# Attention and a squared-ReLU feed-forward: both feed-forward products by Strassen's seven on quarters, two batches a unit

## Chip, cores, metric

One core of one Trainium2 chip. The metric is the time of one execution on the device in microseconds (us), the median of several runs (4 of the kernel before). "PE" is TensorE, "DVE" VectorE, "ACT" ScalarE, "POOL" GpSimd, "SP" SyncE, as in the profile.

## The reference, cut

```python
# q, k, v: 8 batches, 12 heads, 448 rows, 64 columns, float32
q_n, k_n = rmsnorm(q, g_q), rmsnorm(k, g_k)
attn = softmax(q_n @ k_n.T / sqrt(64))
x = (attn @ v)                      # heads side by side: 3584 x 768
h = maximum(x @ w_in, 0)            # 768 x 2048, float64 weights
out = (h * h) @ w_out               # 2048 x 768, float64 weights
```

## The kernel before

A batch's attention goes by pairs of heads (6 pairs, 4 steps each). The feed-forward of batch b-1 is cut into pieces that are issued on PE between the steps of batch b; the last batch's runs alone at the end. The weights arrive as float64 words and are turned into float32 by passes on ACT, POOL and DVE during the first batch and the beginning of the second (the last pass starts at 232.8 us, when the feed-forward already runs); they then stay in SBUF.

```python
for f in range(NF):                                   # first product, 16 tiles of w_in
    ps = banks[6 + f % 2][:, 0:S]
    for c in range(NC):
        nc.tensor.matmul(ps, lhsT=w_in_sb[:, c, ts(f, P)], rhs=xT[c], start=c == 0, stop=c == NC - 1)
    nc.scalar.activation(h[:, at : at + S], ps, AF.Relu)
    nc.gpsimd.tensor_tensor(out=full, in0=full, in1=full, op=ALU.mult)     # (cut: the odd 64 columns)
for n, tt in enumerate(tiles):                        # second product
    for half in range(2):
        ps = banks[6 + half][:, 0:HALF]
        for f in range(NF):
            nc.tensor.matmul(ps, lhsT=h2[f][:, ts(n, P)], rhs=w_out_sb[:, f, ts(half, HALF)], ...)
        # one copy to y, then the store

def convert(k):                                       # one weight chunk
    join_words(k - 1)      # DVE, three passes
    load_weights(k + 3)    # SP
    split_words(k)         # ACT, POOL clamp, ACT, POOL or ACT
```

Of the kernel before, what the change touches and what calls it, by code (L numbers as in the profile page):

```python
# [17 lines left out]
P = 128  # L18


NJ = 4
# [52 lines left out]
def program(ctx, tc, q, k, v, g_row, moe_w_in, moe_w_out, out, shift):  # L74
# [7 lines left out]
    NF = DFF // P  # L82
    HALF = DM // 2
    REST = S % P
    assert 2 * D == P and DM == H * D and B % 2 == 0 and 2 * REST == P and HALF <= 512

# [5 lines left out]
    psum = ctx.enter_context(tc.tile_pool(name="psum", bufs=1, space=bass.MemoryType.PSUM))  # L92

# [4 lines left out]
    w_in_sb = const.tile([P, NC, DFF], F32, name="w_in_sb")  # L98
    w_out_sb = const.tile([P, NF, DM], F32, name="w_out_sb")


# [6 lines left out]
    loaded, values, squared, normal, turned, weights, sums, dens, xts = {}, {}, {}, {}, {}, {}, {}, {}, {}  # L108
# [60 lines left out]
    def turn(i):  # L169

        qn, kn, _ = normal[i]
        qT = att.tile([P, S], F32, name="qT", tag="qT")
        kT = att.tile([P, S], F32, name="kT", tag="kT")
        for x, (dst, rows) in enumerate(((qT, qn), (kT, kn))):
            tr = banks[2 + x][:, 0:S]
            for j in range(NJ):
                nc.tensor.transpose(tr[:, ts(j, CP)], rows[:, j].rearrange("p h d -> p (h d)"), ident[:CP, :CP])  # L177
            if x == 0:
                nc.vector.tensor_scalar(  # L179
                    out=dst, in0=tr, scalar1=g, scalar2=None, op0=ALU.mult  # L180
                )
            else:
                nc.scalar.copy(dst, tr)
        turned[i] = qT, kT
# [5 lines left out]
    def weigh(i, m):  # L190

        if shift:
            return weigh_shifted(i, m)
        new_weights(i, m)
        qT, kT = turned[i]
        scs = [banks[2 * (m % 2) + e][:CP, 0:S] for e in range(2)]
        for e, sc in enumerate(scs):
            r = ds(e * D, D)
            nc.tensor.matmul(sc, lhsT=kT[r, ts(m, CP)], rhs=qT[r, :], start=True, stop=True)  # L199
        for e, sc in enumerate(scs):  # L200
            nc.scalar.activation(  # L201
                weights[i, e, m], sc, AF.Exp, scale=normal[i][2][:, 2 * m + e : 2 * m + e + 1]
            )
        add_up(i, m)

    def add_up(i, m):

        if m == 0 or pairs[i][0] == 0:
            return
        for e in range(2):  # L210
            if m == 1:
                sums[i, e] = att.tile([CP, S], F32, name="sum", tag="sum", bufs=2)
            so_far = weights[i, e, 0] if m == 1 else sums[i, e]
            engine = nc.gpsimd if e == 0 else nc.vector
            engine.tensor_tensor(out=sums[i, e], in0=so_far, in1=weights[i, e, m], op=ALU.add)  # L215

    def weigh_shifted(i, m):
# [4 lines left out]
        qT, kT = turned[i]  # L222
        for e in range(2):
            r = ds(e * D, D)
            sc = banks[2 * e][:CP, 0:S]
# [3 lines left out]
            w = att.tile([CP, S], F32, name="w", tag="w", bufs=1)  # L229
            nc.scalar.activation(w, sc, AF.Exp, bias=nmax)  # L230
            tr = banks[2 * e + 1][:CP, 0:S].rearrange("p (n c) -> p n c", n=NJ)
# [7 lines left out]

    def attend(i, m):  # L240
# [5 lines left out]
        b, c = pairs[i]  # L246
        vt = values[i]
        alone = b == 0
        av = banks[4 + i % 2][:, 0:S]
        den = banks[6 + i % 2 if alone else 5 - i % 2][:, 0:S]  # L250
        for e in range(2):
            nc.tensor.matmul(  # L252
                av[ds(e * D, D), :], lhsT=vt[:, e, m, :], rhs=weights[i, e, m],
                start=m == 0, stop=m == NJ - 1,
            )
        for e in range(2):
            wT = weights.pop((i, e, m))
            if alone:
# [7 lines left out]
        if m == (NJ - 1 if alone else 1):  # L266
# [9 lines left out]

    def finish(i):

        b, c = pairs[i]
        if c == 0:  # L280
            xts[b] = [None] * NC
        xT = ffn_p.tile([P, S], F32, name="xT", tag="xT", bufs=NC + 2)
        nc.vector.tensor_tensor(
            out=xT, in0=banks[4 + i % 2][:, 0:S], in1=dens.pop(i), op=ALU.mult
        )
        xts[b][c] = xT
        del turned[i], normal[i], values[i]



    left = {}

    def out_tiles(b):
        return range(0, S // P) if b % 2 == 0 else range(S // P, 2 * S // P)

    def ffn_pieces(b):
        return NF * 2 + len(out_tiles(b)) * 2 * (NF // 4)

    def ffn(b):

        xT = xts.pop(b)
        at = 0 if b % 2 == 0 else REST
        h2 = []
        for f in range(NF):
            ps = banks[6 + f % 2][:, 0:S]
            for c in range(NC):
                nc.tensor.matmul(  # L307
                    ps, lhsT=w_in_sb[:, c, ts(f, P)], rhs=xT[c],
                    start=c == 0, stop=c == NC - 1,
                )  # L310
                if c == NC // 2 - 1:
                    yield
            if f % 2 == 0:
                two = ffn_p.tile([P, 2, REST + S], F32, name="h2", tag="h2", bufs=NF // 2)
            h = two[:, f % 2]
            nc.scalar.activation(h[:, at : at + S], ps, AF.Relu)  # L316
            if b % 2 == 0:
                rest = ffn_p.tile([P, REST], F32, name="rest", tag="rest", bufs=NF)
                full = h[:, 0 : S - REST]
                over = h[:, S - REST : S]  # L320
                nc.gpsimd.tensor_tensor(out=full, in0=full, in1=full, op=ALU.mult)  # L321
                nc.gpsimd.tensor_tensor(out=rest, in0=over, in1=over, op=ALU.mult)
                left[f] = rest
            else:
                full = h[:, REST : REST + S]
                nc.gpsimd.tensor_tensor(out=full, in0=full, in1=full, op=ALU.mult)  # L326
                nc.gpsimd.tensor_copy(out=h[:, 0:REST], in_=left.pop(f))
            h2.append(h)
            yield
        tiles = out_tiles(b)  # L330
        for n, tt in enumerate(tiles):
            y = ffn_p.tile([P, DM], F32, name="y", tag="y")
            for half in range(2):
                ps = banks[6 + half][:, 0:HALF]
                for f in range(NF):
                    nc.tensor.matmul(  # L336
                        ps, lhsT=h2[f][:, ts(n, P)], rhs=w_out_sb[:, f, ts(half, HALF)],
                        start=f == 0, stop=f == NF - 1,
                    )
                    if f % 4 == 3 and f < NF - 1:  # L340
                        yield
                if half == 0:
                    nc.vector.tensor_copy(out=y[:, ts(half, HALF)], in_=ps)  # L343
                else:
                    nc.scalar.copy(y[:, ts(half, HALF)], ps)  # L345
                    store(b, tt, y)
                yield

    def store(b, tt, y):

        pos = P * tt
        while pos < P * (tt + 1):
            odd, col = divmod(pos, S)
            j, p = divmod(col, CP)
            n = min(CP - p, P * (tt + 1) - pos)
            rows = out[ds((b - b % 2 + odd) * S, S), :].rearrange("(p j) c -> j p c", j=NJ)
            nc.sync.dma_start(rows[j, p : p + n], y[pos - P * tt : pos - P * tt + n, :])
            pos += n



    def weight_chunks():

        n = DFF // 4
        for blk in range(4):
            for c in range(NC):
                yield w_in_sb[:, c, ts(blk, n)], moe_w_in[ts(c, P), :], blk * n
        for half in range(2):
            for f in range(NF):
                yield w_out_sb[:, f, ts(half, HALF)], moe_w_out[ts(f, P), :], half * HALF  # L370

    chunks = list(weight_chunks())
    words = {}

    def load_weights(k):
        if k >= len(chunks):
            return
        dst, rows, col = chunks[k]
        n = dst.shape[1]
        if rows.dtype == F32:  # L380
            nc.sync.dma_start(dst, rows[:, col : col + n])
            return

        early = n == DFF // 4 or k % 2 and k < len(chunks) - NF // 2
        tag, bufs = ("h2", NF // 2) if early else ("y", 2)
        words[k] = ffn_p.tile([P, n, 2], U32, name="words", tag=tag, bufs=bufs)
        nc.sync.dma_start(
            words[k].rearrange("p n w -> p (n w)"), rows.bitcast(U32)[:, 2 * col : 2 * (col + n)]
        )
# [9 lines left out]
    def split_words(k):  # L399
        if k not in words:  # L400
            return
        low, high = words[k][:, :, 0], words[k][:, :, 1]
# [6 lines left out]
        if k < 4 * NC:  # L409
            nc.gpsimd.tensor_scalar(  # L410
                out=low, in0=low.bitcast(F32), scalar1=-(2.0**23), scalar2=1.0,
# [5 lines left out]
    def join_words(k):  # L417
        if k not in words:
            return
# [119 lines left out]
```

## Time and profile before

| | before |
|---|---|
| median | 1717.55 us (4 runs, 1715.78 to 1717.78) |
| span of the profiled run | 1714.3 us |
| first feed-forward matmul | 128.2 us |
| feed-forward alone at the end | from 1552.9 us |

PE is the bound from 128 us on. A line of the page's fifth part reads: source line, engine, operation, output <- inputs, shapes, count, then busy us and mean ns of one, then the engine's idle time before these instructions and who ended it. A matmul of the program is two records in the trace.

### The profile page before, as it was taken

The numbers are of one execution on the slowest core, as the hardware profiler recorded it, in microseconds if no ns is written. First come the engines' busy times: TensorE is split into PE (matmuls) and PEld (weight loads), VectorE is DVE, ScalarE is ACT, GpSimd is POOL, SyncE is SP. The second block draws the span as 40 slices with busy tenths as digits, with TensorE's granted clock in tenths as the row PEclk, the third lists the DMA queues.
The fourth block names the chain that finished last, engine by engine and source line by source line (L and its number), as shares of the span: only waits on it lengthen the run. The fifth ranks groups of instructions, "written<-read, shape, count | busy, mean of one in ns | idle before, by whom it ended". The sixth has DMA issues, their size and how long they took to land.

```text
span 1714.3 us, 14444 instructions
## 1 busy us (share of the span) xinstructions
PE 1649.2 (96%) x5516; PEld 773.9 (45%) x5516; DVE 489.6 (29%) x616; ACT 455.5 (27%) x829; POOL 559.4 (33%) x564
## 2 busy tenths in 40 slices
PE   5879899999999999999999999999999999999998
PEld 2224345444554445534455344444455444454554
DVE  4886731311223122222112222131121312221000
ACT  5666531222113222132111322122211222111100
POOL 5765531333113332233312343133321333211200
PEclk9989999999999999999999999999999999999999
DMA  5533421100011000010010101110001100000000
GB/s 189 187 109 116 122 66 35 42 17 16 26 36 42 16 16 26 26 42 17 17 35 26 42 16 33 35 42 16 16 26 33 43 16 17 15 15 10 0 19 20
DMA packets 80211, 70.24 MB, mean 41 GB/s; under 512 B 47876, under 2 KB 69380, under 8 KB 80132
## 3 DMA queue, kind: packets, MB, share of 16 engines
q1 hardware_dynamic: 80128, 69.23, 13.7%
q8 instruction: 45, 0.74, 0.2%
q14 instruction: 34, 0.28, 0.1%
q10 hardware_dynamic: 4, 0.00, 0.0%
HBM read 58.20 MB, written 11.01 MB: 40 GB/s over the span
## 4 chain that ended last, share of the span: by engine, by line
PE 89%; issue 4%; DVE 4%; POOL 2%; ACT 1%; DMA 0%; POOLq 0%; DVEq 0%; ACTq 0%; SPq 0%
PE bank L336 34%; PE bank L307 32%; PE bank L199 9%; PE bank L252 9%; PE bank L177 2%; PE bank L263 2%; POOL rr L151 1%; DVE w_in_sb L427 1%; DVE sum L215 1%; DVE w_in_sb L423 1%; DVE qT L179 1%; PE bank L259 0%; DVE w_out_sb L427 0%; DMA words<-in_moe_w_out_dram 0%; POOL words L404 0%
## 5 line engine op out<-in xcount | busy, mean ns | idle before, releaser
L307 PE MATMUL bank<-xT,w_in_sb 128*128 128x448 f32 x1536 | 599.9, 545 | 7.6 <-ACT h L316 6.2
L336 PE MATMUL bank<-w_out_sb,h 128*128 128x384 f32 x1792 | 593.9, 489 | 0.0
L336 PEld LDWEIGHTS bank<-w_out_sb,h 128*128 128x128 f32 x1792 | 335.4, 190 | 254.0 <-issue 31.4
L307 PEld LDWEIGHTS bank<-xT,w_in_sb 128*128 128x128 f32 x1536 | 286.6, 191 | 311.7 <-issue 279.1
L201 ACT ACTIVATE wT<-bank,rr 112x448 f32<-112x448 f32 x384 | 222.7, 631 | 547.3 <-PE bank L199 547.3
L199 PE MATMUL bank<-qT,kT 64*112 64x448 f32 x768 | 203.2, 609 | 35.8 <-DVE qT L179 35.2
L252 PE MATMUL bank<-wT,vt 112*64 112x448 f32 x768 | 192.7, 583 | 0.0
L151 POOL TENSOR_TENSOR rr<-ms,minus_half 112x16 f32<-112x16 f32 x48 | 140.4, 2925 | 131.5 <-DVE ms L147 125.4
L316 ACT ACTIVATE h<-bank 128x448 f32<-128x448 f32 x128 | 69.4, 543 | 422.3 <-PE bank L307 422.3
L215 DVE TENSOR_TENSOR sum<-wT 112x448 f32<-112x448 f32 x42 | 26.9, 641 | 539.7 <-PE bank L263 534.6
L215 DVE TENSOR_TENSOR sum<-sum,wT 112x448 f32<-112x448 f32 x84 | 79.8, 950 | 348.3 <-ACT wT L201 348.3
L215 POOL TENSOR_TENSOR sum<-wT 112x448 f32<-112x448 f32 x42 | 66.9, 1592 | 307.4 <-PE bank L263 307.4
L215 POOL TENSOR_TENSOR sum<-sum,wT 112x448 f32<-112x448 f32 x84 | 95.9, 1142 | 194.5 <-ACT wT L201 193.5
L274 DVE RECIPROCAL rden<-bank 128x448 f32<-128x448 f32 x48 | 141.7, 2951 | 6.8 <-PE bank L259 5.6
L326 POOL TENSOR_TENSOR h<-h 128x448 f32<-128x448 f32 x64 | 59.8, 934 | 215.1 <-ACT h L316 215.1
L199 PEld LDWEIGHTS bank<-qT,kT 64*112 64x112 f32 x768 | 55.5, 178 | 152.7 <-issue 93.8
L321 POOL TENSOR_TENSOR h<-h 128x384 f32<-128x384 f32 x64 | 54.2, 847 | 170.4 <-ACT h L316 170.4
L252 PEld LDWEIGHTS bank<-wT,vt 112*64 112x64 f32 x768 | 39.2, 137 | 132.2 <-issue 129.3
L343 DVE COPY y<-bank 128x384 f32<-128x384 f32 x28 | 15.4, 549 | 263.2 <-PE bank L336 263.2
L345 ACT COPY y<-bank 128x384 f32<-128x384 f32 x28 | 13.4, 479 | 216.6 <-PE bank L336 204.0
L146 DVE TENSOR_REDUCE ms<-squares 112x8 f32<-112x512 f32 x96 | 61.3, 679 | 4.4 <-ACT squares L138 4.4
L138 ACT ACTIVATE squares<-qk 112x512 f32<-112x512 f32 x96 | 55.4, 627 | 2.3 <-DMA qk<-in_q_dram 1.4
(41 smaller groups left out, 629.8 us busy)
## 6 DMA issues: line engine op xcount, KB each, us to landing
words<-in_moe_w_in_dram SPq DMA_DIRECT2D x24, 512.0 KB, 4.4
words<-in_moe_w_out_dram SPq DMA_DIRECT2D x32, 384.0 KB, 3.4
qk<-in_q_dram SPq DMA_DIRECT2D x48, 224.0 KB, 2.9
qk<-in_k_dram SPq DMA_DIRECT2D x96, 112.0 KB, 3.3
vt<-in_v_dram SPq DMA_DIRECT2D x48, 224.0 KB, 2.8
out_dram<-y SPq DMA_DIRECT2D x8, 336.0 KB, 2.7
out_dram<-y SPq DMA_DIRECT2D x8, 288.0 KB, 2.6
out_dram<-y SPq DMA_DIRECT2D x8, 240.0 KB, 2.8
```

The lines of the kernel that those rows point to most:

```text
L138: nc.scalar.activation(squares[x], loaded[i][:, x], AF.Square)
L146: nc.vector.tensor_reduce(out=ms[:, ts(x, 2 * NJ)], in_=squares, axis=AX.X, op=ALU.add)
L151: nc.gpsimd.tensor_tensor(out=rr.rearrange("p x r -> p (x r)"), in0=ms, in1=minus_half.to_broadcast([CP, 4 * NJ]), op=ALU.pow,)
L199: nc.tensor.matmul(sc, lhsT=kT[r, ts(m, CP)], rhs=qT[r, :], start=True, stop=True)
L201: nc.scalar.activation(weights[i, e, m], sc, AF.Exp, scale=normal[i][2][:, 2 * m + e : 2 * m + e + 1])
L215: engine.tensor_tensor(out=sums[i, e], in0=so_far, in1=weights[i, e, m], op=ALU.add)
L252: nc.tensor.matmul(av[ds(e * D, D), :], lhsT=vt[:, e, m, :], rhs=weights[i, e, m], start=m == 0, stop=m == NJ - 1,)
L274: nc.vector.reciprocal(out=rden, in_=den)
L307: nc.tensor.matmul(ps, lhsT=w_in_sb[:, c, ts(f, P)], rhs=xT[c], start=c == 0, stop=c == NC - 1,)
L316: nc.scalar.activation(h[:, at : at + S], ps, AF.Relu)
L326: nc.gpsimd.tensor_tensor(out=full, in0=full, in1=full, op=ALU.mult)
L336: nc.tensor.matmul(ps, lhsT=h2[f][:, ts(n, P)], rhs=w_out_sb[:, f, ts(half, HALF)], start=f == 0, stop=f == NF - 1,)
```

## The change

Intent: cut the work of PE. Both operands of a product are split in quarters; Strassen's form (seven products of sums of quarters, in place of eight) cuts 1/8 of the matmuls. The first product is split along the model dimension, the middle dimension and, as rows, into *two batches*: so a unit is two batches. The second works on blocks of the middle dimension, four in a unit, and adds to accumulators in SBUF. The sums of weight quarters ("forms") are made once, written to scratch memory in DRAM and streamed back for every unit. Beside the feed-forward, attention keeps PSUM banks 0 to 3 and the products rotate through 4 to 7. The diff, cut to its core:

```diff
-    w_in_sb = const.tile([P, NC, DFF], F32, name="w_in_sb")
-    w_out_sb = const.tile([P, NF, DM], F32, name="w_out_sb")
+    in_forms = [dram.tile([P, NK, 7, P], F32, ...) for p in range(NF // 2)]
+    out_forms = [dram.tile([P, 8, HALF], F32, ...) for t in range(NF // 2)]
+    ORDER = [("P1", 0, True, "11", "11"), ("P5", 1, True, "S1", "T1"), ("P2", 2, True, "12", "21"),
+        ("P6", 0, False, "S2", "T2"), ("P4", 3, True, "22", "T4"), ("P3", 1, False, "S4", "22"),
+        ("P7", 0, False, "S3", "T3")]          # name, bank, first in it, left and right operand
+    def first_products(u, p, hid):
+        for name, role, first, left, right in ORDER:
+            for c in range(NK):
+                nc.tensor.matmul(roles[role][:, 0:S], lhsT=w_sb[:, c, IN.index(left), :], rhs=forms[u, c][right], ...)
+            # P1, P5, P6, P4: ACT copies the bank; P2, P3, P7: hidden(bank, copy)
+    def hidden(dst, ps, part, op):
+        nc.vector.tensor_tensor(out=dst, in0=ps, in1=part, op=op)
+        nc.scalar.activation(dst, dst, AF.Relu)
+        nc.gpsimd.tensor_tensor(out=dst, in0=dst, in1=dst, op=ALU.mult)
+    def second_products(u, blk, hid, accs):
+        for half in range(2):                  # the leftover tile: 64 rows of each batch
+            for a in range(2):
+                for t in range(2):
+                    nc.tensor.matmul(roles[half][:, 0:HALF], lhsT=flat[a][:, t, ds(FULL, P)], ...)
+            add_to(accs[-1][:, ts(half, HALF)], ps, blk == 0)
+            yield 2 * COST_OUT
+        for dst, left, right, op in (s1, ...), (s2, ...), (s3, ...), (s4, ...):
+            nc.gpsimd.tensor_tensor(out=dst, in0=left, in1=right, op=op)
+        # three row tiles x ORDER x two matmuls; DVE adds each bank to its accumulator
+    def join_words(n):
+        # ... the three DVE passes ...
+        if form == 3:
+            make_weight_forms(...)             # four adds on POOL, then the write to DRAM
     def convert(n):
         join_words(n - 1)
-        load_weights(k + 3)
+        load_weights(n + 4)
         split_words(n)
     # ... in the loop over pairs i and steps n:
-        turn(i + 1)                            # both transposes at step 2
+        if n % 2 == 0 and i < last:
+            turn(i + 1, n // 2)                # qT at step 0, kT at step 2
```

Not shown: batch 1's sums of the softmax go to PE matmuls, as batch 0's did; from batch 2 on the scores use two banks and not four; the loads and the normalization of q and k are issued earlier. All 64 weight pieces are now converted during the attention of batches 0 and 1, with which no feed-forward can be interleaved.

## The prediction

> **What bounds the kernel now.** I read the page of the kernel before first: busy shares, slices, chain.
>
> ```profile
> PE 1649.2 (96%) x5516; PEld 773.9 (45%) x5516; DVE 489.6 (29%) x616; ACT 455.5 (27%) x829; POOL 559.4 (33%) x564
> PE   5879899999999999999999999999999999999998
> ...
> PE bank L336 34%; PE bank L307 32%; PE bank L199 9%; PE bank L252 9%; PE bank L177 2%; PE bank L263 2%; POOL rr L151 1%; DVE w_in_sb L427 1%; DVE sum L215 1%; DVE w_in_sb L423 1%; DVE qT L179 1%; PE bank L259 0%; DVE w_out_sb L427 0%; DMA words<-in_moe_w_out_dram 0%; POOL words L404 0%
> ```
>
> TensorE is full from the fourth slice on, and two thirds of the chain are the two feed-forward products (L307, L336). A busy PE is not a PE at its peak, so I looked for its pace where nothing disturbs it: the chain in order of time ends with one batch's feed-forward alone.
>
> ```profile
> 1552.87 72.36 PE bank L307 x192
> 1625.23 82.57 PE bank L336 x256
> ```
>
> That is 72.36/192 = 0.3769 us for 448 columns and 82.57/256 = 0.3225 us for 384: 2 x 448/2.4 GHz is 373 ns, so this is the floor plus 3 ns. (Each matmul of the program is two records.) By the counts of the page's costliest groups (1536 of L307, 1792 of L336; odd batches have four row tiles, even ones three) all feed-forward costs 1536 x 0.3769 + 1792 x 0.3225 = 579 + 578 = 1157 us.
>
> The windows view tells two stages apart: two whole batches in the middle, then the first 320 us in steps of 20, of which three follow.
>
> ```profile
> 429.31:838.32 409.01, 405.04 (x1362) 190.09 (x1361) 98.90 (x115) 95.41 (x171) 128.51 (x124) 1.00 0.10 27
> ...
> 60.00:80.00 20.00, 15.75 (x70) 4.94 (x68) 18.37 (x22) 13.06 (x24) 15.05 (x12) 0.91 0.52 169
> 80.00:100.00 20.00, 16.93 (x76) 5.42 (x76) 18.58 (x24) 14.08 (x26) 14.51 (x15) 0.91 0.64 209
> ```
>
> In the middle PE is busy 99% and DVE, ACT and POOL 24 to 31%. The period of 409 us for twelve head pairs and two batches of feed-forward (289.3 us) leaves (409.0 - 289.3)/12 = 9.97 us of attention for a pair. In the first 128 us there is no feed-forward to lay between: attention of batch 0 runs beside the conversion of the weights, and DVE is the bound (18.4 of 20 us). The scores' last step of pairs 1 to 6 begins at 41.03, 57.61, 73.22, 89.29, 105.36 and 123.34 in the timeline, some 16.1 us a pair. The first feed-forward matmul is at 128.17.
>
> **What the Trainium skill says.** "TensorE: Matmul & The Clock Gate", section "Wait — 56ns, not 53.3ns?": back-to-back warm matmuls start N/2.4 GHz plus about 2.5 ns apart; the 3 ns above agree, so fewer matmuls are fewer microseconds, one for one. The same page, "What's actually happening": after an idle window of about 3.4 us the array runs at half its clock until busy again about as long. The trace agrees: after 3.07 us idle at 105.36 four score matmuls took 1.84 us in place of 1.01. "DMA: Bandwidth & Descriptors", "Measured": one 1 MB transfer takes 6.15 us, 341 GB/s. The kernel before has none over 512 KB, but a slice of its first 150 us reaches 353 GB/s. "GPSIMD Engine Reference", "Elementwise — side-by-side cycle accounting": a two-input add is about twice as slow on GpSimd as on DVE; here 1142 against 950 ns, less than that.
>
> **The change part by part.**
>
> *Products.* A unit is two batches, so four units. First product: 8 column pairs x 7 products x 3 matmuls x 2 records x 4 units = 1344 records in place of 1536. Second: per block 3 row tiles x 7 x 2 plus 8 for the leftover tile = 50 matmuls, x 4 blocks x 2 records x 4 units = 1600 in place of 1792. At the pace above 1344 x 0.3769 + 1600 x 0.3225 = 506.5 + 516 = 1022 us: -135 us. All of it is on the path. (The leftover tile has no Strassen, so the second product saves 1/9.3, not 1/8.)
>
> *Where the feed-forward starts.* With two-batch units nothing can be laid beside the attention of batches 0 and 1, and all 64 weight pieces of 128x384 are now converted there, 4/3 a step, 5.33 a pair. Loads per pair from the rows by shape: ACT 8 x 0.631 exp + 2 x 0.577 squares + 0.53 = 6.7, plus 5.33 x (0.557 + 0.551 + 0.565) = 8.9 as its third step of every piece is on ACT now: 15.6 us. DVE 2.95 + 1.28 + 0.19 + 0.67 + 0.62 = 5.7, plus 5.33 x (0.392 + 0.637 + 0.683 = 1.71) = 9.1: 14.8 us. POOL 4.0 plus 5.33 x (0.646 + about 0.85 for one 384-wide form) = 8.0: 12.0. PE: eleven. DMA: solving the DMA shares of the first and middle windows for packets, I estimate 0.15 us of one engine for 3 KB, 0.05 for 1 KB, 0.03 for 256 B; a pair then has about 2980/13 = 230 engine-us with the new writes of the forms, /16 = 14.3 us. So ACT, DVE and DMA are all near 15. One saturated engine reached 92% before (14.7 of 16.07); with three I choose 17.6 us a pair. Pair 0 ends its scores near 26 us as before; 11 x 17.6 = 194 gives 220; pair 12, without conversion, about 10; the first load of forms cannot leave before its slot in the queue and adds about 6, the cold clock 2: first feed-forward matmul near 238, +110 us. Attention of 35 pairs in place of 41 is then left for the PE-bound part: 6 x 9.97 = -60. Net +50.
>
> *New waits of PE.* (a) The leftover tile needs the last squared hidden tile: after P7 two DVE passes (0.62 each), relu 0.54, square 0.93 and some 0.4 of hand-overs are 3.1 us, three matmuls (1.9 us) cover it: 1.2 us a block where no attention lies between, more where POOL is in a 2.9 us pow: 16 blocks, +18 us. (b) Attention has banks 0 to 3 only, scores always in 0 and 1: in the four steps of a unit without feed-forward PE waits for exp, some 0.4 us a step, +5. Beside feed-forward (5.8 us a step) it is hidden. (c) P1 to P6 and P6 to P7 share a bank with two products (2.58 us) between; a DVE pass of 0.55 or an ACT copy of 0.5 fits, and even behind a 2.95 us reciprocal it just fits: 0. (d) All seven accumulators leave at the end: +4. The other added work (DVE 90 adds x 0.54 + 32 x 0.62 = 69 us a unit, POOL 32 squares, 16 sums, 12 forms near 70) leaves both under 50% of a unit: 0.
>
> *Weights.* 23.6 MB a unit at 375 us is 63 GB/s, in the last unit 23.6/256 = 92 GB/s. A 1.4 MB load takes near 6 us and has one column pair, 15.8 us, of lead: hidden. Dens of batch 1 by matmul: in the part that PE does not bound.
>
> Sum: 1714.3 - 135 + 50 + 18 + 5 + 4 - 6 (a hole of the conversion near 210 us that goes) = 1650 of span, and the metric is 3.5 us above it: **1654 us**, 3.7% faster.
>
> **The rivals.** *First: the start eats the gain.* If ACT, DVE and the ring of DMA take turns, or the 448 KB of q and k, now behind 1.5 MB writes in the same ring, come late, a pair takes 20 us: +26 us, 1680. For it: three loads near 15 us, DMA at over 80%. Against: the loads are issued four pieces and two steps ahead. *Second: the hand-overs bound the products.* Each group is 4 to 6 records now, not 12 to 32, and nearly each has a reader on DVE or ACT which the next but two must wait for. If a third of 592 groups lost 0.3 us, +60: 1714, and the cold clock could add to it. For it: in-order DVE with 2.95 us reciprocals. Against: the middle has DVE at under half, and the last unit has none. *Third: better than I think.* ACT holds 96% (16.2 us a pair, -15) and attention covers the leftover waits (-12): 1627. *Fourth: streaming is not hidden*: a late in-load stalls PE by microseconds for each of 32 column pairs. Against: 63 to 92 GB/s beside the 353 reached.
>
> **Range and chances.** The saving of matmuls is sure to a few us. The start is uncertain by 15 down and 26 up, the waits by 15 down and 30 up (40 if the second rival is partly true), independently: 1627 to 1690. 2% is 1683.4; I give the sum of both upward errors 12% to pass it, 1% to end over 1752.
>
> **What would show it.** Right: 1344 and 1600 records at the same pace; the last unit's chain near 256 + 5 us from the last attention to the last product; a middle unit near 375 + 5 us; the first product at 230 to 250 us, with ACT and DVE about 85 to 90% busy before; waits of PE on POOL hidden tiles near 1 us each. Wrong: a first product later than 265 us, or PE waiting for DVE or ACT in the middle by over 30 us in sum, or for forms from DMA more than once.

## More of the kernel before

The chain of work that ended last, by engine (the page's fourth part):

```profile
PE 89%; issue 4%; DVE 4%; POOL 2%; ACT 1%; DMA 0%; POOLq 0%; DVEq 0%; ACTq 0%; SPq 0%
```

## The result and the profile after

| | before | after |
|---|---|---|
| median | 1717.55 us | 1767.77 us (4 runs, 1766.04 to 1768.57) |
| ratio | | 1.0293 (1.0275 to 1.0311) |
| records of the feed-forward on PE | 1536 + 1792 | 1344 + 1600 |
| first feed-forward matmul | 128.2 us | 303.2 us |
| last unit or batch alone, from | 1552.9 us | 1494.0 us |
| mean granted clock | 0.985 | 0.952 |

Ratios are the mean time of one kernel's fast runs over that of the other's of the same rounds, so not quite the ratio of the medians. The change made the kernel 2.9% slower; 3.7% faster had been predicted.

The page of the changed kernel: busy shares, PE's slices and granted clock, and the shares of the chain that ended last.

```profile
PE 1578.4 (89%) x5204; PEld 718.9 (41%) x5204; DVE 747.0 (42%) x1082; ACT 551.8 (31%) x1033; POOL 708.2 (40%) x578
...
PE   4766765999998989999998989999998999999997
...
PEclk9888887999999999999999999999999999999999
...
PE 73%; POOL 11%; DVE 6%; issue 5%; DMA 2%; ACT 2%; SPq 1%; POOLq 0%; DVEq 0%; ACTq 0%
```

Two things differ from before. The part in which PE is not full is seven slices of 44 us long; before it was three, of 43 us. And POOL, which was 2% of the chain, is 11% of it. PE's work did shrink, from 1649 to 1578 us of busy time; it is the waiting that grew.

I set the three stages beside the steps of the prediction:

| stage | predicted | measured | difference |
|---|---|---|---|
| until the first feed-forward matmul | 238 | 303.2 | +65 |
| three units beside 35 pairs of attention | 353 + 767 + 17 = 1137 | 1190.8 | +54 |
| last unit alone | 261 | 262.1 | +1 |
| from the last matmul to the end | 10 | 10.4 | 0 |

(The 1137 is made of the prediction's own numbers: 35 pairs at 9.97 us and 4 us for the pair still unfinished, three quarters of 1022, and three quarters of the 23 us of waits of its points a and b. These stages add up to 1646; its own sum, taken as differences from the kernel before, is 1650.) So the floor of PE was right: where nothing comes between, the last unit's chain shows 84 records of the first product in 31.78 us and 84 of the second in 27.09 us, 0.378 and 0.3225 us each.

**The start.** This is the stage from 50 to 270 us in one window (start:end, length, then busy us of PE, PE weight loads, DVE, ACT and POOL, PE's clock, DMA share, GB/s).

```profile
50.00:270.00 220.00, 150.23 (x578) 47.53 (x576) 143.20 (x214) 140.32 (x278) 125.43 (x133) 0.82 0.66 212
```

PE 68%, DVE 65%, ACT 64%, POOL 57%, DMA 66%: no engine is full, yet nothing else runs. The prediction had ACT and DVE near 85 to 90%. The loads themselves it had about right: at the 21.6 us a pair found below these shares are 14.1 us of DVE (14.8 predicted), 13.8 of ACT (15.6), 12.3 of POOL (12.0) and 14.3 of DMA (14.3). The chain in order of time (start us, us, what) shows how they take turns; L558, L562 and L566 are DVE's joins, L583 the four form adds, L542 POOL's clamp.

```profile
229.80 0.57 DVE in_sb L566
230.37 0.07 issue
230.44 1.01 POOL in_sb L583
...
231.53 1.05 POOL in_sb L583 x2
...
233.43 0.99 POOL in_sb L583
234.42 0.50 POOL words L542
234.92 0.02 issue
234.94 0.56 DVE in_sb L558
...
235.53 0.77 DVE in_sb L562
...
236.42 0.57 DVE in_sb L566
236.99 0.04 DVEq L558
237.03 0.49 DVE xT L292
237.52 0.60 DVE qT L187
238.12 0.04 issue
238.16 1.84 PE bank L205 x4
```

Read from the end: PE's scores wait for qT; qT stands in DVE's queue behind xT and the join of a piece; the join waits for that piece's clamp; the clamp stands in POOL's queue behind four form adds; and these had to wait for the join of the piece before. POOL's own work in this is 4.5 us, of which the clamp needs 0.5. PE then also finds its clock halved: four score matmuls take 1.84 us, where others take 1.01. Three pairs took 238.16 - 173.30 = 64.9 us, 21.6 us a pair; 17.6 had been predicted.

**The middle.** PE's waits from 303 us on, in sum, with count and the longest:

```profile
PE bank L420 <- POOL hid L404: 31.5, 16, 4.3
PE bank L448 <- POOL sums L438: 19.1, 6, 6.8
PE bank L383 <- DMA in_sb<-in_forms: 13.1, 1, 13.1
PE bank L383 <- POOL xT L317: 7.9, 2, 3.9
PE bank L260 <- DVE xT L292: 3.7, 3, 2.1
PE bank L185 <- DVE rden L282: 2.5, 2, 1.2
```

The one wait for DMA is the first load, at the end of the start. Without it and the last unit's share of the first line (5.4 us) the middle has 59 us of waits, 53 of them for POOL; the prediction had 17. The timeline of the longest, PE's line first (the bracket is its idle time), then POOL's queue at the same moment:

```profile
649.50 2.93 PE L448 MATMUL bank<-out_sb,sums 128*128 128x384 f32 x4 [6.82 <-POOL sums L438]
```

```profile
641.07 3.21 POOL L161 TENSOR_TENSOR rr<-ms,minus_half 112x16 f32<-112x16 f32 x1 [5.62 <-DVE ms L157]
644.36 1.04 POOL L166 TENSOR_TENSOR qn<-qk,rr 112x512 f32<-112x512 f32 x1
645.35 1.13 POOL L220 TENSOR_TENSOR sum<-wT 112x448 f32<-112x448 f32 x1
646.56 1.13 POOL L223 TENSOR_TENSOR sum<-sum,wT 112x448 f32<-112x448 f32 x1
647.64 1.80 POOL L438 TENSOR_TENSOR sums<-hid 128x768 f32<-128x768 f32 x1
```

The operands of the sum L438 were ready at 635.45, when the last square ended. POOL sat idle for 5.62 us waiting for the attention's mean squares, did a pow and three more things of the attention, and only then the sum PE needed. The Trainium skill's page "Perfetto Trace Analysis", section "Tensor Engine Instruction (MATMUL, LD_WEIGHTS)", says that ACT, DVE and GPSIMD are strict FIFO; the trace agrees, with 12.2 us between the ready operands and the start of an add that takes 1.8.

### The profile page after: what moved, and what is told of

The parts are those of the page before. It is cut to its first block, busy times and chain, and to the rows that moved or that the text cites. A ratio compares the mean times of both kernels' runs of the same rounds, so it can differ in the third digit from the quotient of the medians.

```text
span 1766.5 us, 15113 instructions
## 1 busy us (share of the span) xinstructions
PE 1578.4 (89%) x5204; PEld 718.9 (41%) x5204; DVE 747.0 (42%) x1082; ACT 551.8 (31%) x1033; POOL 708.2 (40%) x578
## 4 chain that ended last, share of the span: by engine, by line
PE 73%; POOL 11%; DVE 6%; issue 5%; DMA 2%; ACT 2%; SPq 1%; POOLq 0%; DVEq 0%; ACTq 0%
PE bank L383 28%; PE bank L448 25%; PE bank L205 8%; PE bank L260 7%; PE bank L420 3%; POOL rr L161 3%; PE bank L185 2%; POOL hid L404 2%; PE bank L271 1%; DVE rden L282 1%; POOL in_sb L583 1%; DMA out_dram<-acc 1%; POOL out_sb L583 1%; POOL words L542 1%; POOL sum L223 1%
## 5 line engine op out<-in xcount | busy, mean ns | idle before, releaser
L383 PE MATMUL bank<-xT,in_sb 128*128 128x448 f32 x1344 | 531.2, 550 | 21.0 <-DMA in_sb<-in_forms 13.1
L383 PEld LDWEIGHTS bank<-xT,in_sb 128*128 128x128 f32 x1344 | 252.6, 192 | 274.4 <-issue 239.9
L404 POOL TENSOR_TENSOR hid<-hid 128x448 f32<-128x448 f32 x128 | 119.1, 941 | 576.8 <-ACT hid L403 576.8
L480 DVE TENSOR_TENSOR acc<-acc,bank 128x384 f32<-128x384 f32 x324 | 173.6, 550 | 273.5 <-PE bank L448 176.9
L448 PE MATMUL bank<-out_sb,hid 128*128 128x384 f32 x768 | 275.6, 488 | 0.0
L448 PE MATMUL bank<-out_sb,sums 128*128 128x384 f32 x576 | 215.7, 498 | 19.1 <-POOL sums L438 19.1
L402 DVE TENSOR_TENSOR hid<-bank,part 128x448 f32<-128x448 f32 x128 | 76.5, 618 | 348.9 <-PE bank L383 325.7
L448 PEld LDWEIGHTS bank<-out_sb,hid 128*128 128x128 f32 x768 | 145.8, 191 | 104.0 <-issue 6.4
L448 PEld LDWEIGHTS bank<-out_sb,sums 128*128 128x128 f32 x576 | 106.1, 192 | 103.8 <-POOL sums L438 22.8
L403 ACT ACTIVATE hid<-hid 128x448 f32<-128x448 f32 x128 | 72.3, 577 | 239.7 <-DVE hid L402 239.7
L420 PE MATMUL bank<-out_sb,hid 128*128 128x384 f32 x256 | 95.9, 521 | 31.5 <-POOL hid L404 31.5
L223 DVE TENSOR_TENSOR sum<-sum,wT 112x448 f32<-112x448 f32 x72 | 76.9, 1068 | 77.1 <-ACT wT L207 73.8
L223 POOL TENSOR_TENSOR sum<-sum,wT 112x448 f32<-112x448 f32 x72 | 81.7, 1135 | 64.3 <-ACT wT L207 61.4
L420 PEld LDWEIGHTS bank<-out_sb,hid 128*128 128x128 f32 x256 | 50.4, 202 | 76.0 <-POOL hid L404 41.3
```

Source lines behind the costliest of these rows:

```text
L223: engine.tensor_tensor(out=sums[i, e], in0=sums[i, e], in1=weights[i, e, m], op=ALU.add)
L383: nc.tensor.matmul(ps, lhsT=w_sb[:, c, IN.index(left), :], rhs=forms[u, c][right], start=first and c == 0, stop=c == NK - 1, skip_group_ch ...
L402: nc.vector.tensor_tensor(out=dst, in0=ps, in1=part, op=op)
L404: nc.gpsimd.tensor_tensor(out=dst, in0=dst, in1=dst, op=ALU.mult)
L420: nc.tensor.matmul(ps, lhsT=flat[a][:, t, ds(FULL, P)], rhs=w_sb[t][:, 2 * a + half, :], start=a == 0 and t == 0, stop=a == 1 and t == 1,)
L448: nc.tensor.matmul(ps, lhsT=lefts[left][:, t, ts(tt, P)], rhs=w_sb[t][:, OUT.index(right), :], start=first and t == 0, stop=t == 1, skip_g ...
```

## The experiments

The theories. **A** (start): the form adds stand ahead of the clamps in POOL's queue. Against it **D**, the DMA ring is full of the form writes, and **C**, the conversion is simply too much work. **B** (middle): the order of POOL's and PE's queues makes the waits, not the work. Medians in us, ratio to before of the same rounds:

| run | median | ratio | first product at |
|---|---|---|---|
| after | 1767.77 | 1.0293 | 303.2 |
| e1_forms_after_clamp | 1744.90 | 1.0166 | 281.2 |
| e2_no_form_writes (wrong result) | 1763.64 | 1.0275 | 300.0 |
| e4_squares_on_act | 1744.95 | 1.0167 | 303.1 |
| e5_leftover_order | 1733.88 | 1.0102 | 303.1 |
| e7_turn_one_step | 1764.51 | 1.0278 | 302.7 |
| e8_sums_before_leftover | 1741.73 | 1.0145 | 303.2 |
| e6_four_edits | 1694.22 | 0.9869 | 265.3 |
| e9_six_edits | 1665.89 | 0.9704 | 262.7 |
| e12_qk_step_earlier | 1656.32 | 0.9639 | 253.5 |
| e10_six_no_writes (wrong result) | 1656.78 | 0.9645 | 252.1 |
| e11_six_no_conversion (wrong result) | 1594.13 | 0.9281 | 195.3 |
| e13_qt_on_act | 1654.01 | 0.9635 | 251.2 |

All others are correct. "Less" below is against 1767.77, which was measured in other rounds; the kernel before, which ran in all, has medians from 1716.36 to 1717.83 in them, so a difference of some 2 us between rounds says nothing. Of the correct versions only e9, e12 and e13 are faster than the kernel before by over 2%.

**e1_forms_after_clamp.**

```diff
     def convert(n):
-        join_words(n - 1)                  # ends with the forms of a finished weight
+        join_words(n - 1)
         load_weights(n + 4)
         split_words(n)
+        while ready:
+            make_weight_forms(*ready.pop())
```

> Edit: the four adds that make a weight form (and the write of the form) are issued after the clamp of the next piece, not before it; nothing else. Theory A (the start is late because 4 us of form adds stand in GpSimd's queue ahead of the next clamp, DVE waits in order for that clamp, and qT behind it): the first feed-forward matmul comes 25 to 45 us earlier than 303 us, DVE's waits for L542's clamp (68 us in the stage) fall by over half, total near 1735. Theory D (the DMA ring is the bound in the start): within 8 us of 1768. Theory C (ACT and DVE simply have too much work there): within 8 us of 1768. The middle is the same under all three.

Measured: 23 us less, all of it before the first product; 20.1 us a pair (nine pairs between the waits for qT at 59.94 and 240.79 us). DVE's waits for the clamp fell from 61 us (60 to 303 us) to 26 (60 to 265 us), in total, with count and the longest, first in the changed kernel, then here:

```profile
DVE out_sb L558 <- POOL words L542: 36.4, 12, 6.8
DVE in_sb L558 <- POOL words L542: 24.5, 6, 4.6
```

```profile
DVE out_sb L558 <- POOL words L542: 18.1, 11, 2.9
DVE in_sb L558 <- POOL words L542: 7.8, 6, 1.4
```

The first product comes 22.0 us earlier, just under the 25 to 45 that A expected, and far over the 8 of C and D. So A is a cause, for a third of the 65 us. PE's clock stayed low and PE still waited some 5 us a pair for qT.

**e2_no_form_writes.**

```diff
-        nc.sync.dma_start(home, dst)
+        nc.sync.dma_start(home[0:1], dst[0:1])
-            nc.sync.dma_start(in_sb[n], in_forms[...])
+            nc.sync.dma_start(in_sb[n], <as many bytes of q>)
```

> Wrong result on purpose: of each form only one partition is written to scratch memory, and the loads of forms read as many bytes of q in their place, so 23.5 of the start's some 58 MB are gone, and nothing else. Theory D (DMA ring): the first feed-forward matmul comes at least 30 us earlier, total under 1740. Theories A and C: under 10 us earlier.

Measured: 4 us less, the first product 3.2 us earlier. D falls: with nearly all of the 23.5 MB of writes gone the DMA share from 50 to 270 us went from 0.66 to 0.41, and the start stayed as it was.

**e4_squares_on_act.**

```diff
-        nc.gpsimd.tensor_tensor(out=dst, in0=dst, in1=dst, op=ALU.mult)
+        nc.scalar.activation(dst, dst, AF.Square)
```

> Edit: the hidden tiles are squared on ACT (Square after Relu) and not on GpSimd. Theory B (of the middle's extra 53 us most are PE waiting for GpSimd, whose queue has 3 us pows, sums and forms ahead of the squares and the Strassen sums): PE's waits for POOL hid (31.5 us) become waits for ACT of some 15 to 20 us, those for POOL sums (19.1 us) fall under 8, total 15 to 30 us less, 1738 to 1753. Rival (the order of DVE, or the shared banks, is behind them): less than 8 us change. The start should not move.

Measured: 23 us less, none in the start. PE's waits at the leftover tile fell from 31.5 to 19.6 us, none over 1.5. Those for the Strassen sums hardly moved (18.8), against the expectation: it was not the squares that stood ahead of them. The waits explain 12 of the 23 us. The rest is the pace of PE: the windows view gives it 1131.7 us of busy time in the changed kernel's middle (303.19 to 1494.07 us) and 1120.9 here (303.10 to 1471.85), for the same 3761 records. The same place in both kernels shows how (the ten records after the wait, first in the changed kernel, then here):

```profile
941.95 5.86 PE L420 MATMUL bank<-out_sb,hid 128*128 128x384 f32 x10 [4.34 <-POOL hid L404]
```

```profile
931.18 3.49 PE L420 MATMUL bank<-out_sb,hid 128*128 128x384 f32 x10 [1.07 <-ACT hid L404]
```

After 4.34 us of idle the same ten matmuls took 5.86 us, after 1.07 us 3.49. There were three waits of that length, and what follows them ran slow too. This is the half clock of the page "TensorE: Matmul & The Clock Gate" (section "What's actually happening") at work: in these traces an idle stretch of that length cost some microseconds more than itself.

**e5_leftover_order.**

```diff
-        for half in range(2):
-            for a, t in (0, 0), (0, 1), (1, 0), (1, 1): matmul into roles[half]
-            add_to(...)
+        for last_one in range(2):
+            for half in range(2):
+                for a, t in ((1, 1),) if last_one else ((0, 0), (0, 1), (1, 0)): matmul into roles[half]
+                if last_one: add_to(...)
+            if last_one: yield 4 * COST_OUT      # was a yield to attention after each half
```

> Edit: in the leftover tile the two matmuls that need the last hidden tile are issued after the six that do not (in both banks), so 3.9 us of matmuls cover the hand-over of 3.3 us and not 1.9. Theory: in the last unit the four waits of 1.36 us go to 0 (-5.4 us); in the middle the twelve waits fall from 26 us to about 8; total -15 to -25 us, 1743 to 1753. If the waits are for POOL's queue by several us, the middle gains less than 8 us and only the last unit gains.

Measured: 34 us less, more than expected. In the last unit the chain of the changed kernel, then that of this run:

```profile
1494.07 31.78 PE bank L383 x84
...
1525.95 0.64 DVE hid L402
...
1526.60 0.59 ACT hid L403
...
1527.26 1.83 POOL hid L404 x2
...
1529.14 3.49 PE bank L420 x10
1532.63 27.09 PE bank L448 x84
```

```profile
1466.87 31.77 PE bank L383 x84
1498.63 5.16 PE bank L420 x16
1503.79 27.09 PE bank L450 x84
```

The hand-over DVE, ACT, POOL (3.3 us) is off the chain: three of the five matmuls that used to stand behind it are now ahead of it. Over the whole kernel the wait fell from 31.5 to 7.2 us, 24 of the 34; PE's busy time in the middle fell by another 8 us (1131.7 to 1123.4, 303.11 to 1466.87 us) for the same records. No work was removed and none moved to another engine. The two yields to attention in this tile became one, so in the middle attention also falls elsewhere; the last unit, which has no attention, is free of that.

**e8_sums_before_leftover.** The four sums of the block are issued on POOL ahead of the leftover tile's code:

```diff
+        for dst, left, right, op in (s1, ...), (s2, ...), (s3, ...), (s4, ...):
+            nc.gpsimd.tensor_tensor(out=dst, in0=left, in1=right, op=op)
         for half in range(2):                  # the leftover tile, with its yields to attention
             ...
-        for dst, left, right, op in (s1, ...), (s2, ...), (s3, ...), (s4, ...):
-            nc.gpsimd.tensor_tensor(out=dst, in0=left, in1=right, op=op)
```

> Edit: the four Strassen sums of the hidden block are issued on GpSimd before the leftover tile's matmuls, not after them, so that no pow and no attention sum gets in front of them; nothing else. Theory B (GpSimd's order): PE's waits for POOL sums (19.1 us in six waits, up to 6.8) fall under 4 us, and the half clock after the two long ones goes too: total -18 to -28, 1740 to 1750. If GpSimd is simply busy there: less than 8 us.

Measured: 26 us less, and the line of 19.1 us is gone from PE's waits; the others are as before. Another 8 us are PE's busy time in the middle, 1123.8 us here. B holds: POOL has the time, its order did not give it.

**e7_turn_one_step.**

```diff
-                if n % 2 == 0 and i < last:
-                    turn(i + 1, n // 2)
+                if i < last and not alone(i + 1):
+                    if n % 2 == 0:
+                        turn(i + 1, n // 2)
+                elif n == 1 and i < last:
+                    for x in range(2):
+                        turn(i + 1, x)
```

> Edit: while attention runs alone, both transposes of the next pair are issued after the scores of step 1, not after those of steps 0 and 2, so the bank of qT is not asked for by the very next scores; nothing else. Theory F (each pair of the start loses time because PE waits 4 to 9 us for qT, which stands behind the reciprocal and the joins in DVE's queue, and its clock halves after that): PE's waits for qT in the start (67 us) fall under 20, the period of 21.6 us a pair falls by 1.5 to 3 us, first feed-forward matmul at 270 to 287 us and not 303, total 1735 to 1752. Rival A (the period is set by the ring of GpSimd's clamps and DVE's joins, and PE's wait is only its shadow): the waits move elsewhere, the start gains less than 8 us. The middle is unchanged.

Measured: 3 us less. F, which I had formed on PE's waits for qT, is not borne out by this edit alone. From 20 to 300 us PE waited 57.6 us for qT still, and 24.5 us for ACT's exp; and from 60 to 250 us ACT now waited 25.4 us for q and k from DMA. The waits moved round the ring of engines, as the rival said. The test is not clean, though: in the changed kernel ACT had no such wait for q and k, the edit brought it about, and e12 mends it.

**e6_four_edits** is e1, e4, e5 and the first loads of forms issued a pair earlier:

```diff
                 elif u == 1 and step == 0:
+                    for t in range(2): load_in(t)      # was at step 4, with load_out between
                     convert(piece)
+                    for t in range(2): load_out(t)
```

> Edits together: forms after the clamp (-23 alone), squares on ACT (-23 alone), leftover order (-34 alone), and the first loads of forms issued a pair earlier (the first product waits 13 us for them: up to -10). If the second and third are mostly the same wait, -23 - 37 - 8: about 1699; if all four add up, 1678. Start: first feed-forward matmul near 272 us.

Measured: 74 us less than after, nearer to the 1699 of one shared wait than to 1678. The first product is 15.9 us earlier than in e1, where PE had waited 16.2 us for the load in e1; two waits of 5.1 and 2.4 us (for a reciprocal and for the T forms) follow it now and give some of that back.

**e9_six_edits** adds e7 and e8.

> The four edits and the two of e7_turn_one_step and e8_sums_before_leftover. From e6 near 1699, another 15 to 25 us for the start and 15 to 22 for the sums: 1655 to 1670, 3% under the kernel before. If the start does not answer to the transposes: 1680.

Measured: 28 us less than e6, in the range, but not as expected: the middle has gained 25.5 us (sums), the start 2.6 and not 15 to 25. In 60 to 250 us ACT waited 22 us for q and k: the load stands where its buffer used to come free, and the transposes now free it a step earlier.

**e12_qk_step_earlier** is e9 with this:

```diff
-                if n == NJ - 1 and i + 3 <= last:
+                if n == (2 if i < last and alone(i + 1) else 3) and i + 3 <= last:
                     load_qk(i + 3)
```

> e9_six_edits and one more: in the start the loads of q and k are issued a step earlier (their buffer is free since the transposes moved). In e9 ACT waited 22 us for them at the squares, at the moments when e7 and e9 lost what the transposes had gained. If these waits set the pair's period there: first product at 245 to 256 us and not 262.7, total 1653 to 1660. If the period is set by the joins of DVE (busy 80%) anyway: within 4 us of 1666.

Measured: 1656.32 us, ratio 0.9639 (0.9623 to 0.9655): 9.2 us in the start. One middle unit (from one wait for DVE to the same wait of the next unit, 629.18 to 1008.63) takes 379.5 us; in the changed kernel it is 402.6 us (649.50 to 1052.14), and 409.0 in the kernel before. The start of this run in two windows:

```profile
50.00:150.00 100.00, 72.25 (x292) 23.76 (x290) 87.09 (x118) 72.86 (x145) 68.73 (x70) 0.85 0.80 255
150.00:240.00 90.00, 60.97 (x252) 20.13 (x254) 75.14 (x101) 62.25 (x124) 64.42 (x64) 0.83 0.71 231
```

DVE is at 87 and 83% now, no longer 65: one engine is nearly full. But ACT waits too: from 60 to 250 us 32 us for the words of the weights from DMA (18.3 + 14.1), where in the changed kernel it was 2.7. Their loads stand in SP's queue behind the writes of the forms (L588), and these wait there 107 us in all for the form adds and the joins.

**e10_six_no_writes** is e12 with the edit of e2.

> Wrong result on purpose: e12 with the form writes cut to one partition and the loads of forms reading q. Now that GpSimd's order is mended the DMA ring may be the next bound of the start. Theory D2 (ring): first product 10 to 25 us earlier than in e12. Rival (DVE's joins): under 5 us.

Measured: the first product 1.4 us earlier, the time the same. With the DMA share down from 0.80 to 0.48 in the first of those windows, DVE is at 88%. The ring, as a carrier of bytes, is not the bound here either. The write itself stays in its place in SP's queue, in e2 as here; whether this order costs time no run tests.

**e11_six_no_conversion** is e12 with the three ACT passes, the clamp and two of three joins taken out.

> Wrong result on purpose: e12 with the conversion of a weight piece cut to one DVE pass (no ACT pass, no clamp, no joins; the same DMA, the same forms). It measures what the conversion costs the start when nothing but attention and forms is left: PE needs 11.2 us a pair, so with waits 13 to 15: first product at 190 to 210 us, total near 1605. If the start is bound by something else (DMA ring, forms), it stays over 235 us.

Measured: first product at 195.3 us, 58 us earlier. So in e12 the conversion (C) holds up the start. The run takes away its work, its hand-overs and the waits of the writes for it, all at once, so it doesn't say which of them. With it gone the first 100 us are:

```profile
50.00:150.00 100.00, 90.43 (x426) 30.39 (x427) 60.73 (x87) 46.68 (x84) 67.18 (x54) 0.93 1.04 341
```

PE is busy 90%, and DMA has a share of 1.04 at 341 GB/s. A pair takes some 14.5 us ((195.3 - 26 - 10)/11, by the prediction's way of counting), near the 14.3 us that it had estimated for DMA. Which of the two bounds the start then isn't shown: the chain from 50 to 195 us lies for two thirds on PE and for a quarter on loads (17% v, 8% words).

**e13_qt_on_act** is e12 with qT copied by ACT in the start.

```diff
+        if x == 0 and alone(i):
+            nc.scalar.activation(dst, tr, AF.Copy, scale=g)
```

> e12_qk_step_earlier and one more: while attention runs alone qT is copied out of its bank by ACT (73% busy) and not by DVE (87% busy), so it no longer stands behind the reciprocal and the joins. If DVE's queue is what is left of the start's delay: PE's waits for qT (22 us in e12 before 250 us) go, the first product comes 5 to 15 us earlier than 253.5, total 1642 to 1652. If the joins of DVE themselves set the pace (its load falls only by 0.7 us of some 19 a pair) and PE's waits are a shadow: within 4 us of 1656.

Measured: 1654.01 us, within the second branch. PE's waits for qT before 250 us are down to one (9.2 us), those for ACT grew from 34 to 41 us (20 to 250), DVE stays at 86% from 50 to 150 us. So PE's waits for qT were a shadow; that the joins of DVE set the pace fits, but is not shown against SP's order (see e12). It is the fastest correct version of these, 3.65% under the kernel before (ratio 0.9635, 0.9619 to 0.9651), though not clear of e12.

## Why the prediction was wrong, point by point

- *Products, -135 us on the path*: right in count and pace (1344 and 1600 records; last unit 262.1 against 261 us).
- *"17.6 us a pair" in the start*: this failed. The step put three loads near 15 us beside each other and set the pair at 13% over the largest of them. The loads were about right; the pair took 21.6 us with no engine over 68%. What it missed is in whose queue the new work stands: the form adds were counted as load on POOL (12 of 17.6 us), not as 4 us in front of the clamp on which DVE, then PE, then ACT wait. Put behind the clamp (e1) they cost 22 us less. The rest of the 65 us in the order in which it was mended: 16 us by the position of the first loads (predicted as a 6 us wait; 8 of the 16 remain after the two waits that follow in e6), 3 with the transposes (e7's edit, in e9), 9 with the q and k loads that these allow (e12). Then the first product is at 253, 15 us over the prediction, and what holds it there is the conversion (e11), with DVE at 83 to 87%, near the predicted 85 to 90, and ACT at 69 to 73, below it.
- *Rival 1, "the start eats the gain"*: right in kind; its size (20 us a pair) was too small and its reason half right. The engines did take turns, but POOL was the third and not DMA (e2, e10); q and k came late only after e7's edit, not in the changed kernel.
- *Point a, leftover tile*: the 3.1 us of hand-over and the 1.2 us of wait are right (3.3 and 1.36 in the last unit); the 18 us in all were 31.5, as POOL's attention work got in front of the squares by up to 3 us, and the half clock after them was left out (PE's busy time in the middle shrank by 11 us with e4 and by 8 with e5).
- *"The other added work ... leaves both under 50% of a unit: 0"*: this is the second step that failed. POOL was at 41% of a middle unit (163.67 of 402.64 us), as counted, and still cost PE 19.1 us at the sums and 7.9 at the T forms. A share says nothing of how long one instruction stands behind others.
- *Point b, scores waiting for exp, +5*: not seen; no such wait is in PE's list. *Point c*: right, no wait between products that share a bank. *Point d*: right.
- *Rival 2, hand-overs bound the products*: partly. The waits were for POOL and not, as it had it, for DVE's reciprocals; 24 of them, up to 6.8 us, not 200 of 0.3.
- *Weights hidden*: right after the first load; no later wait for forms.

Two small readings: the 3.5 us from span to metric set one run's span against the median of others; within a run it is 1.8 (1716.1 to 1714.3). And the add on GpSimd was compared on one form alone; in the same page the other has 1592 ns on POOL against 641 on DVE.

Sum of the edits: e9, e12 and e13 end within 12 us of the predicted 1654, and e12's middle (1390.6 - 253.5 = 1137.1 us) is the predicted 1137. The prediction had nearly the time of a well-ordered version of the change, not of this one. That e13 has 1654.0 is partly luck: its start is 13 us later than predicted, its last unit some 5 us shorter as the leftover waits are gone, and the prediction's sum is 4 us over its own stages.

Open: how much of the start's delay is the half clock by itself. The granted clock stays at 0.81 to 0.86 there in the runs whose windows were read, e11 (0.91 to 0.93) apart, and no run took it away alone. Open too: what the order of SP's queue costs in e12, where word loads stand behind writes that wait.

## What to carry to other kernels

When work moves to engines that "have time", look at where it stands in their queues: what is emitted ahead of an instruction on which another engine waits can be on the path, at whatever share of busy time (POOL's was 57% in the start here, 41% in the middle). Move the waiting consumers apart first: the three purely re-ordering edits (forms, leftover tile, sums) were worth 23, 34 and 26 us here, without a single operation less. Here queues that fed each other in a ring showed as a stage in which no engine was over 68% busy.

## What the Trainium skill lacked or had wrong

- "Perfetto Trace Analysis", section "Identifying the Most-Contended Engine", has the engine of the highest occupancy optimized first. In the start of the changed kernel that was PE with 68%, and re-ordering POOL's queue alone gave 22 us (e1). The page does tell you to look for gaps and for what they wait for; it does not say that the order in which independent work is put into a strict-FIFO queue can be what they wait for.
- "TensorE: Matmul & The Clock Gate", section "What's actually happening", has the half clock come after an idle window of about 3.4 us. In the kernel before it also came after shorter gaps, and not after each: after 1.99 us idle at 954.16 four score matmuls took 1.84 us, after the same 1.99 us at 545.15 1.01 us; after 3.07 us at 105.36, where the prediction saw agreement, 1.84. So the length of a gap alone did not decide it.
- "GPSIMD Engine Reference", section "Elementwise — side-by-side cycle accounting", has a two-input add about twice as slow on GpSimd as on DVE. For the attention sums of 112x448 in the changed kernel the first add took 1129 ns against DVE's 615, the later ones 1135 against 1068: the ratio was 1.8 and 1.06. Why isn't shown.
- "DMA: Bandwidth & Descriptors", section "Measured", gives 6.15 us and 341 GB/s for 1 MB, for transfers issued from GpSimd; 1 MB in 6.15 us is 170 GB/s, half of that. Here SP issues them: the 1344 KB loads of forms landed in a median of 5.8 us (237 GB/s); of the 1536 KB ones, issued two at a time, the median was 9.3 us.
